# A new order of the items of phase one in a fused attention and MoE kernel

## The chip, the core and the metric

The kernel runs on one core of a Trainium2 chip. The metric is the time of one execution on the device in microseconds. All operands are f32. The engines are called by their names in the profile: PE is TensorE (matmuls; PEld is its weight loads), DVE is VectorE, ACT is ScalarE, POOL is GpSimd and SP is SyncE, which here only issues DMA transfers.

## The reference: what is computed

Attention with pooled keys and values, whose output is the input of an "act-snake" layer. There are 8 batches, 8 heads, 576 positions and 64 values a head; the layer has 4608 tokens, a model width of 512 and an inner width of 2048.

```python
k_p = k.reshape(B, H, Sp, pool, D).mean(axis=3)          # pool = 8, Sp = 72
v_p = v.reshape(B, H, Sp, pool, D).mean(axis=3)
scores = scale * np.matmul(q, k_p.transpose(0, 1, 3, 2))
scores = scores - np.max(scores, axis=-1, keepdims=True)
attn = np.exp(scores)
attn = attn / (np.sum(attn, axis=-1, keepdims=True) + 1e-09)
x = np.matmul(attn, v_p)                                 # heads side by side: 4608 x 512
h = x @ w_in                                             # 512 x 2048
g = h + np.sin(alpha * h) ** 2 / (alpha + 1e-09)
out = g @ w_out                                          # 2048 x 512
```

## The kernel before

**Two phases.** Phase one (to some 509 us) computes attention and g and writes g to a tensor in HBM, `g_bridge`. Phase two reads g back and multiplies it with w_out; its code is `outputs`, its matmuls stand at L1294.

**Phase one: units and groups.** The tokens are taken in nine units u of 512. In each unit there are four groups J, one for each quarter of the inner width; group number n is 4u + J. A group computes its part of h by a scheme of Strassen's kind: seven products M1 to M7 of sums of blocks of x and w_in instead of eight, each in four parts ("M5.2" is a part; one matmul call of 128 x 128 weights and 256 columns at L975, which PE runs as two instructions). Four PSUM banks collect them. "c16" and "c67" are ACT copies from one bank into another (L950), because a later product is added to an earlier sum; "p5" is an ACT copy of M5's bank into SBUF. DVE forms the other blocks of h ("a00", "a01", "a11", L949). ACT applies the sine ("s00", "s01", "s10", "s11", L1044, two instructions each) and squares ("q00", "q01", "q1", L1051), DVE adds the square to h ("f10", "f1", L949), and SP stores the group's g with two DMAs of 512 KB ("st", L1099).

In units 1 to 6, except in the first group of unit 1, some products (M5 for J = 0, 2, 3; M1 for every J) are themselves computed by seven smaller products: items "i.a" to "i.e5". PE's parts of these are matmuls of 128 columns at L1066; between them ACT copies ("i.ca" L1079, "i.cm" L1083, "i.cb" L1086) and one DVE add ("i.ad", L1089). The order of dependence is i.a, then i.ca and i.cm, then i.b, i.cb, i.d, then i.ad, which reads the bank that i.d has finished, and then i.e1 and i.e5, which add to what i.ad wrote.

**Attention, spread between the groups.** While unit u's groups run, the attention of batch u + 1 and the loads for batch u + 2 go along, item by item (`carry`). The items of one batch:

- load_k0, load_k1 (L261, 576 KB each), load_v (L280 and L285), load_q (L224, L245): DMAs on SP's queue. pool_k0, pool_k1, pool_vm, pool_v: sums of 8 rows on POOL (L271).
- qa, qb, qc: DVE transposes of q, 32 by 32 (L357, L360). qd, qe: eight DMAs each on SP that move the transposed blocks to their partitions (L370, `q<-tr`). k_t and k_c: a PE transpose of the pooled k and its DVE copies (L402, L406).
- scores0, scores1: PE's products of q and k (L444). shift0 to shift3: DVE maximum and subtraction (L464, L465). exp0 to exp3: ACT (L490). norm0 to norm3: DVE and POOL (L496 to L498).
- turn0 to turn3: DVE transposes of the weights (L630 to L636). move: sixteen DMAs on SP (L650, `ex<-tr`). values: PE's products with v (L739, L752). out0 to out4: ACT writes the result into x (L666). sx0 to sx3: DVE differences of blocks of x (L939) for M5, M6, M7 and M4 of the next unit. inner_x: such differences for the inner products, on POOL (L931).

Unit 0 carries the end of batch 0 and batch 1, with items of its own; there the differences are called sn0 to sn3.

**What sets the order.** The kernel sets the order by hand. Each item has a slot in a table, and a key is made of it; a list of all items is sorted by key and performed in that order, and each engine's queue holds its instructions as they come. Nothing reorders them afterwards: an engine that waits for one instruction holds all that stand behind it. Semaphore waits follow from the data.

```python
self.at(7 * n + where[m], f)          # group n: where = ORDER[self.kind(n)]
at(ORDER["U"][name], f)               # unit u: key 28 * u + slot
self.agenda.sort(key=lambda x: x[:2])
```

So four groups of 7 fill a unit of 28, and slots can be below 0 or above 7: parts of neighbouring groups interleave. The tables: "U" is the unit's items for u from 1 on, "U0" those of unit 0, "F" the first batch, "U7" the differences in the last but one unit, "R" the preparation of phase two and its first steps ("o0" to "o2", the start of `outputs`, whose key is 224 plus the slot; so "o1" is at 249.65, where the last group, number 35, has its slot 4.65). The groups' tables are chosen by `kind`: "first0" to "first3" for unit 0, "enter" for the first group of unit 1, "mid0" to "mid3" for the other groups up to unit 6, "exit" for the last group of unit 6, "end0" to "end3" for units 7 and 8.

Of the kernel before, what the change touches and what calls it, by code (L numbers as in the profile page):

```python
# [46 lines left out]
    "load_q": 13.4176, "load_k1": 13.54022, "turn0": 15.964, "move": 24.04575, "clean": 24.12855, "qa": 24.12869, "values": 24.12873,  # L47
    "out4": 24.12875, "qb": 24.12884, "pool_k1": 24.12885, "out0": 24.12885, "mark": 24.12895, "qc": 24.129, "out2": 24.129, "sx0": 24.1291,
    "inner_x": 24.12915, "out3": 24.33175, "k_t": 24.4364, "k_c": 24.4956, "qd": 24.83712, "out1": 24.87145, "sx1": 24.87995, "qe": 24.96216,
    "sx2": 25.5786, "sx3": 33.62096},  # L50
# [56 lines left out]
"enter": {  # L107
# [6 lines left out]
"exit": {  # L114
    "i.a": -5.02158, "i.ca": -4.768, "i.cm": -4.76115, "i.b": -4.15145, "i.cb": -3.5502, "i.d": -3.09985, "i.ad": -3.09835, "i.e1": -2.6215,
# [1455 lines left out]
```

## Time and profile before

| | us |
|---|---|
| median of 3 runs (904.27 to 905.8) | 905.39 |
| span of the profiled execution | 902.2 |
| PE busy | 894.0 |
| PEld busy (beside PE) | 815.0 |
| DVE busy | 678.2 |
| ACT busy | 457.3 |
| POOL busy | 206.5 |

The profiled execution's span runs from its first to its last instruction; the timed runs are 3.2 us longer in the median, which is start and end outside of the span. Busy times of the engines lie beside each other. The profile page's chain of waits goes back from the last instruction to what released it; a group's row gives busy time, mean duration in ns and idle time before it with the releaser; a line of the waits gives the waiting engine, line and tile, the releaser, the sum in us, the count and the longest. In a timeline a line has start, duration, engine, line, tiles, count. SPq lines are DMA issues; their duration is the time to issue, not to land.

In stages of about 55 us, one unit each, between 134 and 409 us, PE is busy throughout by its row, DVE 35.9 to 39.4 us, ACT 42.3 to 44.0 and POOL 16.6 to 23.6 us, the DMA engines 0.52 to 0.70 of the time. The granted PE clock is 1.00 in all of them.

### The profile page before, as it was taken

How to read it: one execution, taken by the hardware profiler on the slowest of the kernel's cores; microseconds unless marked ns; L12 is line 12 of the kernel's file. 1: busy time of each engine (PE TensorE's matmuls, PEld its weight loads, DVE VectorE, ACT ScalarE, POOL GpSimd, SP SyncE). 2: the span in 40 equal slices, each digit the busy share in tenths (PEclk: the TensorE clock that was granted, in tenths of full speed). 3: DMA queues.
4: the chain of work that ended last, by engine and by line, in shares of the span. 5: the costliest groups of instructions: out<-in, count | busy, mean ns of one | idle time of the engine just before them, and what ended most of it. 6: DMA issues, size and time to landing. Idle time of an engine off the chain costs nothing.

```text
span 902.2 us, 18350 instructions
## 1 busy us (share of the span) xinstructions
PE 894.0 (99%) x7146; PEld 815.0 (90%) x7146; DVE 678.2 (75%) x1016; ACT 457.3 (51%) x1073; POOL 206.5 (23%) x235
## 2 busy tenths in 40 slices
PE   8999999999999999999999999999999999999997
PEld 5787888978888898888888899999999999999997
DVE  7576857668586684854466999979798888889894
ACT  5696878868787787786885611211111111111111
POOL 4969561814418164130000000000000000000000
PEclk9999999999999999999999999999999999999999
DMA  9956766666766666645426346261618172534401
GB/s 271 229 170 181 209 193 177 209 173 200 212 179 197 198 187 173 175 133 200 181 104 213 99 152 193 65 191 35 224 30 231 31 201 63 171 92 130 134 15 40
DMA packets 128751, 141.17 MB, mean 156 GB/s; under 512 B 46920, under 2 KB 95704, under 8 KB 128664
## 3 DMA queue, kind: packets, MB, share of 16 engines
q1 hardware_dynamic: 125880, 137.88, 52.6%
q10 hardware_dynamic: 2784, 2.11, 0.9%
q8 instruction: 57, 0.93, 0.4%
q14 instruction: 30, 0.25, 0.1%
HBM read 75.37 MB, written 47.19 MB: 136 GB/s over the span
## 4 chain that ended last, share of the span: by engine, by line
PE 98%; DVE 1%; DMA 0%; ACT 0%; issue 0%; ACTq 0%
PE PS L1294 43%; PE PS L975 41%; PE PS L1066 7%; PE PS L444 2%; PE PS L739 2%; PE PS L752 1%; DVE home L939 1%; DMA q<-in_q_dram 0%; PE PS L553 0%; PE PS L532 0%; PE PS L1131 0%; PE PS L416 0%; PE PS L697 0%; PE PS L343 0%; PE PS L695 0%; PE PS L607 0%
## 5 line engine op out<-in xcount | busy, mean ns | idle before, releaser
L975 PE MATMUL PS<-home,a 128*128 128x256 f32 x968 | 250.3, 382 | 0.0
L975 PEld LDWEIGHTS PS<-home,a 128*128 128x128 f32 x968 | 177.3, 190 | 28.6 <-issue 4.7
L975 PE MATMUL PS<-home,as 128*128 128x256 f32 x728 | 194.9, 381 | 0.9 <-DVE home L939 0.9
L975 PEld LDWEIGHTS PS<-home,as 128*128 128x128 f32 x728 | 134.1, 190 | 18.3 <-DVE home L939 0.9
L1294 PE MATMUL PS<-s,wb 128*128 128x144 f32 x896 | 119.1, 286 | 0.0
L1294 PEld LDWEIGHTS PS<-s,wb 128*128 128x128 f32 x896 | 113.6, 190 | 0.0
L1051 ACT ACTIVATE s<-s,c 128x256 f32<-128x256 f32 (+1 forms) x216 | 112.7, 580 | 0.0
L1344 POOL TENSOR_TENSOR cc<-cc,cb 128x576 f32<-128x576 f32 x1 | 2.0, 1974 | 483.1 <-DVE cb L1249 483.1
L949 DVE TENSOR_TENSOR h<-PS,s 128x512 f32<-128x512 f32 x72 | 49.5, 687 | 70.3 <-ACT s L1051 70.3
L1430 ACT COPY PS<-PS 128x144 f32<-128x144 f32 x56 | 14.7, 263 | 143.4 <-PE PS L1294 140.8
L1294 PE MATMUL PS<-r,wb 128*128 128x144 f32 x512 | 73.2, 286 | 0.0
L1294 PE MATMUL PS<-s,a 128*128 128x144 f32 x512 | 73.2, 286 | 0.0
L1044 ACT ACTIVATE s<-h,al 128x256 f32<-128x256 f32 x144 | 64.1, 502 | 16.4 <-DVE h L949 13.3
L271 POOL TENSOR_TENSOR kvin<-kvin 96x768 f32<-96x768 f32 (+3 forms) x42 | 69.9, 1665 | 3.1 <-DMA a<-in_moe_w_in_dram 0.6
L1294 PEld LDWEIGHTS PS<-r,wb 128*128 128x128 f32 x512 | 67.1, 190 | 0.1
L1294 PEld LDWEIGHTS PS<-s,a 128*128 128x128 f32 x512 | 67.1, 190 | 0.0
L949 DVE TENSOR_TENSOR h<-PS,p 128x512 f32<-128x512 f32 x72 | 49.1, 685 | 22.3 <-PE PS L975 21.7
L950 ACT COPY PS<-PS 128x512 f32<-128x512 f32 x72 | 41.4, 576 | 46.2 <-PE PS L975 23.0
L1044 ACT ACTIVATE s<-PS,al 128x256 f32<-128x256 f32 x144 | 60.3, 473 | 6.1 <-PE PS L975 5.8
L498 POOL TENSOR_TENSOR ex<-ex,sm 128x576 f32<-128x576 f32 (+1 forms) x28 | 35.2, 1270 | 109.8 <-DVE sm L497 108.9
L1412 ACT COPY PS<-PS 128x144 f32<-128x144 f32 x56 | 14.7, 263 | 88.7 <-PE PS L1294 88.7
L949 DVE TENSOR_TENSOR h<-h,s 128x1024 f32<-128x1024 f32 x36 | 44.8, 1246 | 14.2 <-ACT s L1051 14.1
(217 smaller groups left out, 1531.4 us busy)
## 6 DMA issues: line engine op xcount, KB each, us to landing
g_bridge<-h SPq DMA_DIRECT2D x72, 512.0 KB
r<-g_bridge SPq DMA_DIRECT2D x31, 1152.0 KB
out_dram<-o SPq DMA_DIRECT2D x122, 72.0 KB
kvin<-in_k_dram SPq DMA_DIRECT2D x14, 576.0 KB
q<-in_q_dram SPq DMA_DIRECT2D x7, 1024.0 KB
kvin<-in_v_dram SPq DMA_DIRECT2D x14, 512.0 KB
ex<-tr SPq DMA_DIRECT2D x54, 92.0 KB
ex<-tr SPq DMA_DIRECT2D x54, 88.0 KB
```

The source lines that it names most:

```text
L271: self.nc.gpsimd.tensor_tensor(out=t[..., 0:w] if w > D else out, in0=t[..., 0:w], in1=t[..., w:2 * w], op=OP.add)
L444: nc.tensor.matmul(ps[e][r0 + r:r0 + r + q.shape[-1], h, :], q[s], kb[s, hp, :], start=True, stop=True)
L498: nc.gpsimd.tensor_tensor(out=E(i), in0=E(i), in1=sm.unsqueeze(2).to_broadcast([P, n, Sp]), op=OP.mult)
L739: nc.tensor.matmul(o[r:r + 64], w, x, start=start and i < 2, stop=False, skip_group_check=True)
L949: add = lambda o, x, y: nc.vector.tensor_tensor(out=o, in0=x, in1=y, op=OP.add)
L950: copy = lambda o, x: nc.scalar.copy(out=o, in_=x)
L975: nc.tensor.matmul(ps[:, jj, :], self.A[p][:, kk, f * P:(f + 1) * P], x[:, kk, :], start=start and p not in G.begun, stop=(kk == 1), skip_ ...
L1044: self.nc.scalar.activation(out=G.s()[:, i, jj, j, :], in_=src[:, jj], func=AF.Sin, scale=self.al[:, f:f + 1])
L1051: self.nc.scalar.activation(out=x, in_=x, func=AF.Square, scale=self.c[:, f:f + 1])
L1066: nc.tensor.matmul(out, W[m][:, G.J], self.X2[p][m], start=start, stop=True, skip_group_check=True)
L1294: nc.tensor.matmul(out, W[:, J // 2, J % 2, :], A[:, J, :], start=(start and J == 0), stop=(J == self.NJ - 1), skip_group_check=True)
L1412: nc.scalar.copy(out=st["x1"][:, 1, :], in_=st["x1"][:, 0, :])
```

## The change

Only numbers in the table ORDER are new: those of "U", "end0" to "end3", "enter", "exit", "first0" to "first3" and "mid0" to "mid3". Names, operations, tiles and transfers stay. "F" (the first batch), "U0", "U7" and "R" keep their numbers. The program has the same instructions in both versions, 541 DMAs on SP and 13 on ACT, apart from the waits on semaphores between them (PE 254 and then 252, ACT 291 and 279, DVE 321 and 330, POOL 111 and 110, SP 181 and 184). The changed file is ten lines longer within the table, so that L975 becomes L985 and so on.

Two of the places in words. In "U" the DMA moves qd and qe, both at about 24.9 before, stand at 24.3 and 29.1: between them now come two stores ("st" of a group) and load_k0 of the next batch (at -2.8 of the next unit, 25.2 here). In "mid3" and "exit" as in the others, i.e1 and i.e5 stand further behind i.ad than they did.

```diff
 "U": {
-    "load_k0": -3.59252, "load_v": -0.96965, "scores0": 3.279, "shift1": 6.66681, "shift0": 7.14828, "scores1": 7.66855, "shift2": 7.69635,
...
-    "load_q": 13.4176, "load_k1": 13.54022, "turn0": 15.964, "move": 24.04575, "clean": 24.12855, "qa": 24.12869, "values": 24.12873,
-    "out4": 24.12875, "qb": 24.12884, "pool_k1": 24.12885, "out0": 24.12885, "mark": 24.12895, "qc": 24.129, "out2": 24.129, "sx0": 24.1291,
-    "inner_x": 24.12915, "out3": 24.33175, "k_t": 24.4364, "k_c": 24.4956, "qd": 24.83712, "out1": 24.87145, "sx1": 24.87995, "qe": 24.96216,
-    "sx2": 25.5786, "sx3": 33.62096},
+    "load_k0": -2.8250723, "scores0": 0.5857662, "shift1": 1.0717224, "shift0": 1.0827303, "scores1": 8.3882114, "shift2": 10.4991635,
+    "exp1": 11.165643, "exp0": 11.5859082, "shift3": 11.616854, "pool_k0": 11.626981, "exp2": 11.6269842, "exp3": 11.7278035, "load_v": 11.7293126,
...
+    "load_k1": 11.9490121, "turn3": 12.0644122, "turn1": 12.6257197, "load_q": 12.8268737, "pool_k1": 15.0669519, "clean": 15.0933368,
+    "pool_vm": 15.8286396, "pool_v": 17.866474, "move": 20.672534, "qb": 22.3496327, "qc": 24.0548236, "values": 24.0585347, "mark": 24.0662953,
+    "out4": 24.0671002, "out0": 24.0979304, "qa": 24.0981694, "out2": 24.0985162, "out3": 24.1565579, "sx0": 24.2086769, "k_t": 24.2853448,
+    "k_c": 24.2950439, "inner_x": 24.2968397, "qd": 24.3191907, "out1": 24.3619433, "sx1": 24.5667552, "sx2": 25.1581598, "qe": 29.1248421,
+    "sx3": 29.1312358},
...
 "end3": {
...
-    "M4.2": 4.2433, "M4.0": 4.41961, "M4.3": 4.42479, "s01": 4.63625, "s10": 4.64555, "q01": 6.26891, "q1": 6.5869, "f1": 6.76776, "f10": 7.38579,
-    "st": 10.05},
...
+    "q01": 4.3173274, "M4.2": 4.6452332, "s10": 4.64555, "q1": 4.6470475, "f1": 6.6621497, "f10": 7.4423293, "st": 8.2738671},
 "enter": {
-    "M1.0": -0.5012, "M1.2": -0.49378, "M1.1": -0.48667, "M1.3": -0.47146, "M5.0": -0.45225, "M5.1": -0.39509, "M5.2": -0.11055, "M5.3": -0.01999,
-    "c16": 0.2794, "p5": 0.86945, "M6.0": 2.04465, "M2.0": 2.65792, "M2.1": 4.32577, "M2.3": 4.65506, "M6.1": 4.856, "M6.3": 4.86001, "M6.2": 4.87325,
...
+    "M1.0": -0.2046709, "M1.3": -0.1478548, "M1.1": -0.1446769, "M1.2": -0.046174, "c16": -0.0136544, "M5.0": 0.4150293, "M5.3": 0.420676,
+    "M5.1": 0.4360173, "M5.2": 0.4717303, "M6.0": 0.4900667, "p5": 0.5493729, "M6.1": 0.5625392, "M6.3": 1.0762283, "M2.0": 1.79859,
...
 "mid0": {
-    "i.a": -3.44775, "i.ca": -3.11535, "i.cm": -3.1115, "i.b": -3.11065, "i.cb": -3.1106, "i.d": -2.748, "i.ad": -1.9601, "i.e5": -0.69805,
-    "p5": 2.55425, "i.e1": 2.87235, "c16": 2.92563, "M2.3": 5.96454, "M2.2": 5.96455, "M2.0": 5.96456, "M6.2": 5.96456, "M6.1": 6.07936,
...
+    "i.a": -3.6916192, "i.ca": -3.3128811, "i.b": -3.0311432, "i.cb": -2.951107, "i.cm": -2.8418044, "i.d": -2.8417678, "i.ad": -2.8042301,
+    "i.e5": 0.0539427, "i.e1": 0.0748215, "p5": 0.0963461, "c16": 0.5698113, "M2.2": 0.9641797, "M2.3": 0.9877027, "M2.1": 1.0895164,
...
 "exit": {
-    "i.a": -5.02158, "i.ca": -4.768, "i.cm": -4.76115, "i.b": -4.15145, "i.cb": -3.5502, "i.d": -3.09985, "i.ad": -3.09835, "i.e1": -2.6215,
-    "i.e5": -2.5921, "c16": -1.98745, "M6.3": -1.6521, "M6.1": 1.03682, "M2.1": 1.99737, "M6.2": 2.6094, "M2.0": 2.6097, "M6.0": 2.61059,
...
+    "i.a": -5.7170466, "i.ca": -5.1713547, "i.b": -4.2359372, "i.cb": -3.8379418, "i.d": -3.8159482, "i.cm": -3.7995184, "i.ad": -2.9857453,
+    "i.e1": -0.6667843, "c16": -0.2461357, "i.e5": -0.2165688, "M6.2": -0.2019642, "M6.3": -0.1979378, "M2.0": -0.189832, "M6.0": 0.0901443,
...
 "mid3": {
-    "i.a": -5.44769, "i.cm": -5.07042, "i.ca": -4.6089, "i.b": -4.1596, "i.cb": -3.09295, "i.d": -3.08935, "i.ad": -3.08745, "i.e1": -2.73575,
...
+    "i.a": -5.8347122, "i.ca": -5.1713514, "i.cm": -4.8365744, "i.b": -4.1342384, "i.cb": -4.1048847, "i.d": -3.4866891, "i.ad": -3.2781619,
+    "i.e1": -0.8431389, "c16": -0.3116682, "i.e5": -0.2224887, "M6.2": -0.2202882, "M6.0": 0.2738904, "p5": 2.6316117, "M6.1": 2.6333881,
...
```

More of the change, by code (lines that the diff above doesn't have):

```diff
@@ L80 @@
 "end0": {
[26 rows of a table removed]
-"enter": {
[6 rows of a table removed]
-"exit": {
-    "i.a": -5.02158, "i.ca": -4.768, "i.cm": -4.76115, "i.b": -4.15145, "i.cb": -3.5502, "i.d": -3.09985, "i.ad": -3.09835, "i.e1": -2.6215,
[34 rows of a table removed]
-    "i.a": -3.44775, "i.ca": -3.11535, "i.cm": -3.1115, "i.b": -3.11065, "i.cb": -3.1106, "i.d": -2.748, "i.ad": -1.9601, "i.e5": -0.69805,
[6 rows of a table removed]
-    "i.a": 4.34025, "i.ca": 4.3997, "i.cm": 4.40437, "i.b": 4.4051, "i.cb": 4.40681, "M5.0": 4.41522, "i.d": 4.41525, "i.ad": 4.61795,
[6 rows of a table removed]
-    "i.a": -2.3038, "i.cm": -1.76102, "i.ca": -1.7514, "i.b": -1.7503, "i.cb": -1.7501, "i.d": -1.735, "i.ad": -1.59855, "i.e1": -1.0348,
[6 rows of a table removed]
-    "i.a": -5.44769, "i.cm": -5.07042, "i.ca": -4.6089, "i.b": -4.1596, "i.cb": -3.09295, "i.d": -3.08935, "i.ad": -3.08745, "i.e1": -2.73575,
[5 rows of a table removed]
[27 rows of a table added]
+"enter": {
[7 rows of a table added]
+"exit": {
+    "i.a": -5.7170466, "i.ca": -5.1713547, "i.b": -4.2359372, "i.cb": -3.8379418, "i.d": -3.8159482, "i.cm": -3.7995184, "i.ad": -2.9857453,
[37 rows of a table added]
+    "i.a": -3.6916192, "i.ca": -3.3128811, "i.b": -3.0311432, "i.cb": -2.951107, "i.cm": -2.8418044, "i.d": -2.8417678, "i.ad": -2.8042301,
[7 rows of a table added]
+    "i.a": 4.1556036, "i.ca": 4.3387363, "i.b": 4.3596664, "i.cm": 4.503322, "M5.0": 4.5236076, "i.cb": 4.6105216, "i.d": 4.6269693,
[7 rows of a table added]
+    "i.a": -2.2706958, "i.cm": -2.1707003, "i.ca": -2.0398794, "i.b": -2.0163978, "i.cb": -1.8551907, "i.d": -1.2779286, "i.ad": -1.1683365,
[7 rows of a table added]
+    "i.a": -5.8347122, "i.ca": -5.1713514, "i.cm": -4.8365744, "i.b": -4.1342384, "i.cb": -4.1048847, "i.d": -3.4866891, "i.ad": -3.2781619,
[6 rows of a table added]
 }
```

156 rows, old and new, of the table ORDER are left out of this document.

## The prediction

> **What bounds the kernel now.** I read the head of the page and its chain first, then the waits of TensorE and of its weight loads, then the timeline where a wait stands.
>
> ```profile
> span 902.2 us, 18350 instructions
> ...
> PE 894.0 (99%) x7146; PEld 815.0 (90%) x7146; DVE 678.2 (75%) x1016; ACT 457.3 (51%) x1073; POOL 206.5 (23%) x235
> ...
> PE 98%; DVE 1%; DMA 0%; ACT 0%; issue 0%; ACTq 0%
> ...
> L975 PE MATMUL PS<-home,a 128*128 128x256 f32 x968 | 250.3, 382 | 0.0
> ```
>
> TensorE is the bound: 98% of the chain. An f32 matmul runs as two passes, and their starts in the timeline lie 216 ns apart (four of L975 in 0.86 us), so one part of an M product, two matmuls of 256 columns at L975 or four of 128 at L1066, costs 0.43 us whatever its place. The change adds no pass and takes none away. What it can move are holes in the TensorE stream, and those are small: over all of phase one I count 9.9 us of them between starts. The sum is made against the span of 902.2; the median of the three runs, 905.39, is 3.2 more, which lies outside the span and which I leave as it is.
>
> The waits of TensorE's weight loads name the holes:
>
> ```profile
> PEld PS L739 <- issue: 6.7, 27, 0.3
> ...
> PEld PS L1066 <- DVE PS L1089: 4.2, 11, 0.4
> ...
> PEld PS L975 <- ACT PS L950: 1.4, 7, 0.2
> ```
>
> ```profile
> 127.33 1.03 PE L975 MATMUL PS<-home,a 128*128 128x256 f32 x4
> 128.34 0.49 PE L1066 MATMUL PS<-home,aM 128*128 128x128 f32 x2
> 128.66 0.39 PE L1066 MATMUL PS<-ex,a 128*128 128x128 f32 x2
> ```
>
> The second fence (TensorE's timeline) prices one of the eleven: four matmuls from 127.33 should let the next start at 128.19, it starts at 128.34, and its pair takes until 128.66 instead of 128.56. That is 0.15 + 0.10 = 0.25 us; the weight-load row counts more because loads run ahead.
>
> **Gain a, the inner products.** In six units the DVE add L1089 ("i.ad") releases "i.e1" and "i.e5" of L1066. Before, two M parts (the four matmuls from 127.33, 0.86 us) stand between "i.d", whose end starts the add (0.70 us), and the readers. In the new order of TensorE there are three at each of the eleven places. The third is 0.43 us, more than the 0.15 that is missing, and leaves 0.3 spare. 11 x 0.247 = -2.7 us; bounds -2.7 and -1.5, should five of the adds start later behind other DVE work.
>
> **Gain b, copies c67.** Seven waits on L950, each showing 0.06 us on the starts, and one of 0.25 us on an output copy (L666) near 84.5 lose their late releaser. I take -0.6; bounds -0.9 and -0.2.
>
> **Loss c, values.** The new slot puts "values" (L739) directly behind the group's copy p5 (L950, ACT): laid on the rows' durations, the copy ends 0.09 us after TensorE arrives, where it ended 0.27 us ahead. Five units at 0.09 to 0.2 (a lateness costs about 0.1 more, as at 128.34): +0.7, bounds 0 and 1.0. In unit 0 the same comes from copies L666 and L746, 0.32 and 0.09 late: +0.45, bounds 0 and 0.6.
>
> **Loss d, i.ca.** The copy L1079 comes 40 ns ahead of its reader instead of 250; rows with 35 to 75 ns of cover show 0.04 to 0.09 us. Six times 0.05: +0.3, bounds 0 and 0.6.
>
> **Loss e, the first group of unit 1 (near 85 to 92 us).**
>
> ```profile
> 85.02 4.05 DVE L939 TENSOR_TENSOR home<-home 128x512 f32<-128x512 f32 x2 [1.68 <-ACT home L666]
> 89.00 1.75 DVE L939 TENSOR_TENSOR home<-home,home 128x512 f32<-128x512 f32 x1
> ```
>
> ```profile
> 87.45 1.13 PE L975 MATMUL PS<-home,as 128*128 128x256 f32 x4 [0.54 <-DVE home L939]
> ...
> 90.89 0.67 PE L975 MATMUL PS<-home,as 128*128 128x256 f32 x2 [0.33 <-DVE home L939]
> ```
>
> Four differences of x (L939) run one after another beside POOL's sums and take 2.38, 1.75, 1.75 and 1.34 us, where they take 0.69 alone. M5 and M6 of "enter" wait for them. The new table lays an add L949 (0.69) between the first difference and the others, and M6.0 right behind the four parts of M5 (2.04 to 0.49), so 1.7 us of TensorE's work that stood between is gone. By the rows: M5 late 0.15 instead of 0.61, M6 1.62 instead of 0.51; +0.6, bounds 0 and 1.6.
>
> **Loss f, into phase two.**
>
> ```profile
> 514.34 0.38 ACT L1397 COPY PS<-PS 128x288 f32<-128x288 f32 x1
> 514.64 2.13 ACT L1051 ACTIVATE s<-s,c 128x256 f32<-128x256 f32 x4
> ...
> 516.67 0.27 ACT L1430 COPY PS<-PS 128x144 f32<-128x144 f32 x1
> ```
>
> The last group's "q1" moves from slot 6.587 to 4.647. Group 35 begins at key 245, so q1 goes from 251.587 to 249.647, and the first output products ("o1") are at 224 + 25.65 = 249.65: the squares now stand ahead of the copy L1397, not behind it. Its matmuls end as before, so the copy comes about 1.4 us later. One block of TensorE (0.98) has moved between, and 0.34 was spare: 0.09 late; L1430 then 0.54. +0.65, bounds 0 and 1.4.
>
> **Loss g, the moves of q.**
>
> ```profile
> 244.98 10.51 SPq L370 DMA_DIRECT2D q<-tr  x16
> 255.59 1.07 SPq L1099 DMA_DIRECT2D g_bridge<-h  x2
> 256.76 2.25 SPq L280 DMA_DIRECT2D kvin<-in_v_dram  x2
> ```
>
> ```profile
> 256.00:257.00 1.00, 1.00 (x55) 0.92 (x46) 0.91 (x3) 1.00 (x3) 0.00 (x0) 1.00 0.62 197
> 257.00:258.00 1.00, 1.00 (x6) 0.87 (x6) 0.97 (x3) 1.00 (x4) 0.00 (x0) 1.00 1.02 367
> ```
>
> SP issues the sixteen moves ("qd", "qe") in one run, 0.65 us each, then stores and loads. They land 2.0 us after issue by the trace's completions, the last near 257.0; the second half of scores that reads them begins at 260.97: 4.0 us of cover. In the new order qd begins 1.46 us later, since it waits for a DVE transpose ("qa") that has moved behind others; after its eight, SP issues the two stores (1.07 us, 1.05 MB) and load_k0 (0.55 us, 0.59 MB), and then qe. The scores move by 0.4. So by issue times alone 1.3 us of cover is left, 4.0 - 1.46 - 1.62 + 0.4. But the last columns (DMA share, GB/s) show that stores fill the engines (1.02 at 367 GB/s), and transfers of SP's queue land in order of issue: a k load issued at 238.97 landed at 244.1, stores issued behind it at 245.5 and 247.9. Stores and k are 1.64 MB: 4.5 us at 367 GB/s, 5.8 us at 281 (the row from 260 to 261). The eight moves queue up behind them, each 0.25 us of full engines (0.65 us at a share of 0.4, rows 250 to 256). In the first case the queue is empty again when the last is issued and nothing is lost; in the second it lands 1.5 us later than issue gives, 0.2 late; and if k takes the 5.1 us from issue to landing that it took at 238.97, counted from the stores' landing, up to 1.6 late. I take 0.55 late, in each of four units: +2.2, bounds 0 and 6.4.
>
> **Loss h, sx3.** The last difference of x moves from 33.6 to 29.1, beside the POOL sums of pool_k0 (L271). Beside POOL L931, L939 takes up to 1.75; beside L271 the add of two SBUF tiles runs as ever:
>
> ```profile
> L949 DVE TENSOR_TENSOR h<-h,s 128x1024 f32<-128x1024 f32 x36 | 44.8, 1246 | 14.2 <-ACT s L1051 14.1
> ```
>
> Those next to L271 took 1.215. The DVE work behind sx3 (shift L464, L465) has some 0.9 us of cover, and only then the inner products wait. +0.3 in all, bounds 0 and 4 (1.06 longer less 0.16 spare, in four to five units).
>
> The Trainium skill (SBUF — State Buffer, Who interferes with whom) says that a DVE instruction with both inputs in SBUF contends with a GpSimd instruction that reads SBUF. By that rule alone each sx3 would lose the rest of a POOL sum, and the whole change would come to some 911; the trace agrees for L939 beside L931 (1.75 against 0.69) and not for L949 beside L271 (1.215).
>
> Covered, at nothing: the pooling sums, loads of k and v and the softmax steps that move within their unit. DVE is idle about 30% and POOL more than half of each stage (windows of 55 us); their readers come a unit later. If that cover is gone, the price is one waiting stage of 0.5 us per unit, 3 us.
>
> **Sum.** -2.7 - 0.6 + 0.7 + 0.45 + 0.3 + 0.6 + 0.65 + 2.2 + 0.3 = +1.9; 905.39 + 1.9 = 907.3.
>
> **Rivals.**
> 1. The moves land in time (the other side). Loss g is nothing if stores and k go at the upper rate: -0.3, 905.1, no change. It decides as soon as the last move lands less than 1.3 us later than issue alone gives. For it: moves alone fill only 0.32 to 0.65 of the engines (250 to 257), so a block of k can be made up. Against: k loads took 5.1 us.
> 2. Gains only. If moreover the start of L739 (0.25 us in 27 rows, releaser "issue") hides loss c, and d to f come at their low ends: -3.3 + 0.9 = -2.4, 903.0. For it: the lateness of c, 0.09, is less than that start. Against: f needs 1.4 us of squares to vanish.
> 3. The queue costs its upper end. Moves 1.6 us late in four units: 907.3 + 4.2 = 911.5. For it: stores behind a k load needed 5.9 and 7.9 us to land.
> 4. sx3 is blocked. DVE's chain 0.9 late in four units: 907.3 + 3.6 - 0.3 = 910.6; rows of both signs stand above.
> 5. A cover that I count on is gone (above): 907.3 + 3 = 910.3.
>
> **Chances.** Forecast 0.38 (906 to 910, six tenths of it over 907.2), rival 1 0.20, rival 2 0.13, rival 3 0.14, rival 4 0.09, rival 5 0.06. A measurement tells 0.2%, 1.8 us, from no change. Slower by that: rivals 3 to 5 and six tenths of the forecast, 0.52. Faster: rival 2 and some of rival 1, 0.16. Within: 0.32. For 8 in 10 the range runs from just above rival 2 to just past rival 3: 903.2 to 912.0.
>
> **What would show it.** Waits of L1066 on L1089 gone (a); L739 waiting on L950 (c); in 85 to 92 us one wait of 1.6 at M6 (e); L1294 waiting on ACT L1397 and L1430 with 0.6 in all (f); the scores L444 waiting for DMA q<-tr, 0.3 to 0.8 in units 2 to 5 (g); L939 over 1 us once a unit (h). I am wrong if TensorE waits in a place that no part names, above all for pooled k or the transposes of q, or if L444 doesn't wait for DMA at all.

## The result and the profile after

The changed kernel takes 916.36 us in the median (915.36 to 917.02), the kernel before in the same runs 904.84 (904.27 to 905.8). The ratio is 1.0125, with a 95% interval of 1.011 to 1.0139: 11.5 us slower, six times the loss that was forecast (1.9 us), and outside of the range.

The head of the page and the chain of the changed kernel:

```profile
span 915.2 us, 18347 instructions
...
PE 899.5 (98%) x7146; PEld 820.9 (90%) x7146; DVE 687.2 (75%) x1016; ACT 455.2 (50%) x1073; POOL 206.4 (23%) x235
...
PE 79%; DVE 6%; ACT 5%; DMA 4%; SPq 2%; issue 1%; POOL 1%; ACTq 0%; DVEq 0%; POOLq 0%
```

TensorE is still the bound, but only 79% of the chain runs through it where it was 98%; DVE, ACT and DMA have come in. Line numbers are ten higher than before: L985 was L975, L959 was L949.

Its waits, first of the matmuls, then of the weight loads (waiting engine, line, tile, releaser, sum in us, count, longest):

```profile
PE PS L985 <- ACT PS L960: 4.0, 4, 1.2
...
PE PS L454 <- DMA q<-tr: 0.9, 2, 0.6
...
PE PS L1304 <- ACT PS L1440: 0.4, 1, 0.4
PE PS L1304 <- DVE r L1259: 0.3, 1, 0.3
PE PS L1304 <- DVE x L1259: 0.3, 1, 0.3
```

```profile
PEld PS L1076 <- ACT PS L1089: 2.7, 6, 0.5
...
PEld PS L1076 <- DVE PS L1099: 0.3, 1, 0.3
```

The last line is gain a: of eleven waits for the add "i.ad" (4.2 us in the weight-load row before) one is left. The first line is new and was in no part of the prediction: TensorE waits about a microsecond for the copy "c16" (L960, from bank to bank), four times.

Where the time between the two profiled executions goes, from the starts of the matmuls (lateness against the same step elsewhere, the 0.1 us that follows a wait included where it could be separated):

| | us |
|---|---|
| c16: 1.09, 1.21, 0.95, 1.41, 0.27 in five units | +4.9 |
| i.ca (L1089): five times 0.37 | +1.9 |
| second half of scores, units 2 to 5: blocks of 2.85, 2.16, 2.39, 2.19 where they took 1.55 | +3.4 |
| values, units 1 to 5: blocks of 4.52, 3.87, 3.87, 3.88, 3.87 where they took 3.5 to 3.6 | +2.4 |
| values, unit 0: a block of 4.00 where it took 3.42, between starts | +0.6 |
| phase two, first to last matmul: 386.26 instead of 384.10 | +2.2 |
| i.ad: one of eleven waits left | -2.5 |
| first group of unit 1: one wait, 0.77 with its tail, instead of two, 1.38 | -0.6 |
| c67 and the output copy near 84.5 | -0.6 |
| sum | +11.7 |

From the first product to the first matmul of phase two the time rose from 491.6 to 501.2 us, which with phase two makes 11.7. The spans differ by 13.0, because the first product came 1.6 us later in this execution. That isn't the kernel's doing: in the executions profiled for this study it comes at 21.6 to 23.4 us where the order of the kernel before is the base, and at 21.4 to 23.5 where the changed one is. The timed runs lie 1.7 to 2.1 us above their spans, so of the 3.2 us that were put outside of the span before, more than 1 was the difference of that execution from the median; the difference between the kernels doesn't hang on it.

**What makes c16 late.** The timeline of DVE and of POOL around one of these waits, in the changed kernel:

```profile
229.97 0.69 DVE L959 TENSOR_TENSOR h<-PS,p 128x512 f32<-128x512 f32 x1
230.58 3.15 DVE L959 TENSOR_TENSOR h<-h,s 128x1024 f32<-128x1024 f32 x1
233.66 0.68 DVE L959 TENSOR_TENSOR h<-PS,s 128x512 f32<-128x512 f32 x1
```

```profile
229.79 0.43 POOL L516 MEMSET ex<- 32x128 f32 x2
230.30 4.56 POOL L281 TENSOR_TENSOR kvin<-kvin 128x1024 f32<-128x1024 f32 x2
```

and the same place before, again DVE and POOL:

```profile
225.64 1.22 DVE L949 TENSOR_TENSOR h<-h,s 128x1024 f32<-128x1024 f32 x1
```

```profile
225.14 0.61 POOL L291 TENSOR_TENSOR vz<-vr,mask 128x256 f32<-128x256 f32 x1
225.71 3.37 POOL L271 TENSOR_TENSOR kvin<-kvin 128x1024 f32<-128x1024 f32 x1
```

The add "f1" (h plus the squares, both inputs in SBUF) and the first sum of pool_vm (1024 columns, both inputs in SBUF) don't run side by side. Alone they take 1.22 and 2.35 us. Before, f1 starts 0.07 us ahead of POOL: f1 takes 1.22 and POOL's sum 3.37. After, POOL starts 0.28 us ahead of f1: POOL takes its 2.35 (4.56 is two sums), and f1 takes 3.15. Before, f1 led by 0.06 to 0.08 us in four units running. After, it was behind by 0.42, 0.28, 0.56 and 0.09 us in units 1, 3, 4 and 5 and took 3.02, 3.15, 2.88 and 3.34 us. In unit 6 it was behind by 1.23 and took 2.21; that is the unit with the 0.27 us of c16. In unit 2 f1 led by 0.86 us, and there neither c16 nor i.ca made TensorE wait.

The chain of the changed kernel shows how two lost microseconds on DVE come to TensorE:

```profile
230.03 3.71 DVE h L959 x2
233.77 0.64 ACT s L1054 x2
234.58 1.61 ACT s L1054 x4
236.19 1.23 ACT s L1061 x2
237.42 0.48 ACT PS L960
```

Sines and squares on ACT wait for DVE, the copy c16 stands behind them on ACT, and the matmul at 237.95 has waited 1.05 us for it.

**The moves of q**, on SP and then on TensorE, in unit 3:

```profile
195.90 4.67 SPq L380 DMA_DIRECT2D q<-tr  x7
200.62 1.12 SPq L1109 DMA_DIRECT2D g_bridge<-h  x2
201.84 0.84 SPq L271 DMA_DIRECT2D kvin<-in_k_dram  x1
202.72 6.83 SPq L380 DMA_DIRECT2D q<-tr  x8
```

```profile
210.00 0.84 PE L454 MATMUL PS<-kblk,q 64*64 64x72 f32 x34
211.13 1.00 PE L454 MATMUL PS<-kblk,q 64*64 64x72 f32 x46 [0.30 <-DMA q<-tr]
```

The eight last moves are issued behind stores and k, in 6.83 us where eight took some 5.2 before, and the scores stop in mid-block for them.

**Into phase two**, the chain of the changed kernel (pieces of it):

```profile
527.22 0.30 ACT PS L1407
...
528.93 8.38 DMA r<-g_bridge
537.31 0.02 issue
537.33 2.57 DVE x L1259
```

Behind the copies that the prediction named there is a load of r on ACT's own DMA queue. It goes out at 528.93, 4.6 us after phase two's first matmul; before it was at 516.37, 3.2 us after. DVE's sums and then two blocks of TensorE wait for it.

### The profile page after: what moved, and what is told of

Read it like the earlier page. It is cut to its first block, busy times and chain, and to the rows that moved or that the text cites. A ratio compares the mean times of both kernels' runs of the same rounds, so it can differ in the third digit from the quotient of the medians.

```text
span 915.2 us, 18347 instructions
## 1 busy us (share of the span) xinstructions
PE 899.5 (98%) x7146; PEld 820.9 (90%) x7146; DVE 687.2 (75%) x1016; ACT 455.2 (50%) x1073; POOL 206.4 (23%) x235
## 4 chain that ended last, share of the span: by engine, by line
PE 79%; DVE 6%; ACT 5%; DMA 4%; SPq 2%; issue 1%; POOL 1%; ACTq 0%; DVEq 0%; POOLq 0%
PE PS L1304 40%; PE PS L985 29%; PE PS L1076 4%; DVE h L959 3%; ACT s L1054 2%; PE PS L454 2%; DMA kvin<-in_k_dram 2%; ACT s L1061 2%; PE PS L749 1%; SPq L660 1%; SPq L380 1%; DMA r<-g_bridge 1%; POOL kvin L281 1%; PE PS L762 1%; DVE tr L640 1%
## 5 line engine op out<-in xcount | busy, mean ns | idle before, releaser
L985 PE MATMUL PS<-home,a 128*128 128x256 f32 x968 | 249.6, 381 | 4.1 <-ACT PS L960 4.0
L985 PEld LDWEIGHTS PS<-home,a 128*128 128x128 f32 x968 | 179.1, 190 | 32.1 <-ACT PS L960 5.1
L985 PE MATMUL PS<-home,as 128*128 128x256 f32 x728 | 194.0, 382 | 0.5 <-DVE home L949 0.5
L985 PEld LDWEIGHTS PS<-home,as 128*128 128x128 f32 x728 | 132.5, 190 | 17.5 <-ACT s L1054 0.9
L1304 PE MATMUL PS<-s,wb 128*128 128x144 f32 x896 | 119.2, 286 | 0.4 <-ACT PS L1440 0.4
L1304 PEld LDWEIGHTS PS<-s,wb 128*128 128x128 f32 x896 | 113.6, 190 | 0.6 <-ACT PS L1440 0.6
L959 DVE TENSOR_TENSOR h<-PS,s 128x512 f32<-128x512 f32 x72 | 48.7, 687 | 69.1 <-ACT s L1061 69.0
L281 POOL TENSOR_TENSOR kvin<-kvin 96x768 f32<-96x768 f32 (+3 forms) x42 | 71.9, 1712 | 44.0 <-DMA kvin<-in_k_dram 41.4
L959 DVE TENSOR_TENSOR h<-h,s 128x1024 f32<-128x1024 f32 x36 | 52.5, 1458 | 33.4 <-ACT s L1061 33.4
L1304 PE MATMUL PS<-r,wb 128*128 128x144 f32 x512 | 73.3, 286 | 0.3 <-DVE r L1259 0.3
L1304 PE MATMUL PS<-s,a 128*128 128x144 f32 x512 | 73.2, 286 | 0.0
L1304 PEld LDWEIGHTS PS<-r,wb 128*128 128x128 f32 x512 | 67.1, 190 | 0.6 <-DVE r L1259 0.6
L1304 PEld LDWEIGHTS PS<-s,a 128*128 128x128 f32 x512 | 67.0, 190 | 0.0
L960 ACT COPY PS<-PS 128x512 f32<-128x512 f32 x72 | 41.5, 576 | 45.7 <-PE PS L985 22.6
L959 DVE TENSOR_TENSOR h<-PS,p 128x512 f32<-128x512 f32 x72 | 48.7, 684 | 13.5 <-PE PS L985 12.1
L1304 PE MATMUL PS<-x,wb 128*128 128x144 f32 x384 | 55.0, 286 | 0.3 <-DVE x L1259 0.3
```

The lines of the kernel that those rows point to most:

```text
L281: self.nc.gpsimd.tensor_tensor(out=t[..., 0:w] if w > D else out, in0=t[..., 0:w], in1=t[..., w:2 * w], op=OP.add)
L959: add = lambda o, x, y: nc.vector.tensor_tensor(out=o, in0=x, in1=y, op=OP.add)
L960: copy = lambda o, x: nc.scalar.copy(out=o, in_=x)
L985: nc.tensor.matmul(ps[:, jj, :], self.A[p][:, kk, f * P:(f + 1) * P], x[:, kk, :], start=start and p not in G.begun, stop=(kk == 1), skip_ ...
L1304: nc.tensor.matmul(out, W[:, J // 2, J % 2, :], A[:, J, :], start=(start and J == 0), stop=(J == self.NJ - 1), skip_group_check=True)
```

## Experiments

Each kernel is measured against the kernel before in the same job; "before" below is that job's median. Ratios carry their 95% interval.

**POOL's order alone.** The short sums of pool_v go ahead of the long ones of pool_vm, as they did in the kernel before.

```diff
-"pool_vm": 15.8286396, "pool_v": 17.866474,
+"pool_vm": 17.866474, "pool_v": 15.8286396,
```

> The changed kernel with two POOL items exchanged: the short sums of v's last rows (pool_v) ahead of the long sums (pool_vm). Theory (port): the add f1 (L959, two inputs in SBUF, 1.2 us alone, 2.2 to 3.3 us in five units) is held by the 2.35 us sum of pool_vm that began just before it, and the waits of PE for the copies c16 (L960, 4.9 us in sum) and for i.ca (L1089, five of 0.37 us) come of that. Then f1 meets only sums of some 0.5 us and those waits go: 4 to 7 us faster than the changed kernel, some 910 to 912 us. Rival (order): ACT and DVE are late through the new places of the transposes turn0 to turn3, and f1 only waits where something else would: no change, 915 to 917 us.

910.08 us, before 905.51; ratio 1.0052 (1.0039 to 1.0065). f1 takes 1.6 us at most, where it meets the short sums, as here, on DVE and on POOL:

```profile
228.63 1.60 DVE L959 TENSOR_TENSOR h<-h,s 128x1024 f32<-128x1024 f32 x1
```

```profile
228.43 2.52 POOL L281 TENSOR_TENSOR vr<-vr 128x256 f32<-128x256 f32 x3
```

No wait for c16 is left, and of those for i.ca two of 0.04 us and less. The time from first product to phase two falls by 6.6 us. The transposes turn0 to turn3 stand where the change put them, so the rival falls: it is the meeting of the two instructions, not their place in ACT's or DVE's order as such.

**One transpose alone, on the kernel before.** Why did f1 lose its lead? In the changed kernel the 0.9 us of turn0 stand ahead of it, and POOL's two items have changed places. The next kernel does only the first of these to the kernel before.

```diff
-"turn0": 15.964,
+"turn0": 12.95,
```

> The kernel before with one transpose moved as the change moves it: turn0 ahead of the add f1 of mid0, so that f1 comes 0.9 us later on DVE. Theory (who starts first holds the port): before, f1 starts 0.06 to 0.08 us ahead of the 2.35 us sum of pool_vm in four units and takes 1.22 us; now POOL starts first, f1 takes 2.5 to 3.3 us, and PE waits about 1 to 1.5 us a unit for a copy that hangs on it: 4 to 7 us slower than before, 909 to 912 us. Rival (only 0.9 us later): f1's readers have that much cover; less than 1.5 us slower.

915.83 us, before 905.67; ratio 1.0116 (1.0102 to 1.013). One item moved by 0.9 us costs 10.2 us, more than expected. DVE, POOL and TensorE:

```profile
232.24 2.75 DVE L949 TENSOR_TENSOR h<-h,s 128x1024 f32<-128x1024 f32 x1
```

```profile
231.55 4.57 POOL L271 TENSOR_TENSOR kvin<-kvin 128x1024 f32<-128x1024 f32 x2
```

```profile
237.97 0.70 PE L975 MATMUL PS<-home,as 128*128 128x256 f32 x2 [1.21 <-ACT PS L950]
```

f1 is 0.09 us behind POOL in unit 1 and 0.68 in units 2 to 5, takes 3.35 and 2.75 us, and TensorE is 1.97 us late for the copy L950 in unit 1 and 1.38 in each of the others. The rest are seven waits of 0.2 us for the same line, and the 0.1 us that follows each.

**The same with POOL out of the way.**

```diff
-"turn0": 15.964, "pool_v": 11.93269,
+"turn0": 12.95, "pool_v": 11.93271,
```

> The same as the run with turn0 first, and pool_vm ahead of pool_v on POOL, so that its 2.35 us sum is over when f1 starts and f1 meets a sum of 1.27 us half done at most. Theory (port): f1 takes below 1.9 us; at least 3 us faster than with turn0 first alone, 905 to 907.5 us. Rival (0.9 us later): the same time as with turn0 first.

910.22 us; ratio 1.0049 (1.0037 to 1.0062). Against the run before it 5.6 us come back: f1 takes 1.20 in unit 1 and 1.8 in units 2 to 5, where it now starts behind the second sum of pool_vm (512 columns, 1.27 us alone), and TensorE waits 0.43 there instead of 1.38. DVE and POOL (the second sum starts at 227.27):

```profile
227.83 1.79 DVE L949 TENSOR_TENSOR h<-h,s 128x1024 f32<-128x1024 f32 x1
```

```profile
224.83 3.71 POOL L271 TENSOR_TENSOR kvin<-kvin 128x1024 f32<-128x1024 f32 x2
```

Of the 10.2 us, at least 5.6 are thus the held add. The other 4.6 are the 0.9 us of transposes in a place without cover and the 0.6 us for which f1 is still held; this run doesn't separate them. The theory's 905 to 907.5 us was missed, and the rival of that pair may be right for a part.

**The order on SP alone.** qe directly behind qd.

```diff
-"qe": 29.1248421,
+"qe": 24.3192,
```

> The changed kernel with the eight moves qe directly behind qd, ahead of the two stores and of load_k0. Theory (queue): the second half of the scores waits 0.6 to 1.3 us in four units because the moves stand behind 1.64 MB of stores and k on one queue; then these waits go and the kernel is 3.4 us faster, some 913 us. Rival (late start): qd and qe are late because the DVE transpose qa comes later; then at least half of the waits stay, 914.5 us or more.

908.73 us, before 905.51; ratio 1.0038 (1.0026 to 1.005). All second halves of the scores take 1.55 us again, here at the place shown above:

```profile
208.15 1.53 PE L454 MATMUL PS<-kblk,q 64*64 64x72 f32 x80
```

That is the 3.4 us, and the rival falls, since qd begins as late as in the changed kernel (14.6 us ahead of this block in both). The gain was larger, 7.6 us between the medians and 6.1 in the profiled execution (the twelve runs spread from 905.67 to 910.9), because with SP's order POOL's start moved too: f1 led by 0.61 and 0.21 us in units 4 and 5 and took 1.2 us there.

**ACT's order alone.** q1 of end3 behind the first output products.

```diff
-"q1": 4.6470475,
+"q1": 6.5869,
```

> The changed kernel with q1 of end3 back at slot 6.587, behind the first output products. Theory (ACT's queue): both the copies L1407 and L1440 and the load of r that ACT issues behind them come earlier; the waits of PE for the copies (1.0 us) and for x and r of L1259 (1.2 us) all go: 2.2 us faster, some 914.2 us. Rival (copies alone): the load of r is late through the stores on SP; only the 1.0 us goes, 915.4 us.

914.58 us, before 905.51; ratio 1.0096 (1.008 to 1.0111). Phase two takes 384.19 us again, 2.07 less, and all four waits of L1304 are gone. The load on ACT's queue goes out 3.3 us after the first matmul of phase two, as before:

```profile
527.55 0.26 ACT L1440 COPY PS<-PS 128x144 f32<-128x144 f32 x1
527.58 0.40 ACTq L1250 DMA_DIRECT2D r<-g_bridge  x1
```

**Three parts undone together** (pool_v ahead, qe ahead, q1 back).

> The changed kernel with three parts undone: pool_v ahead of pool_vm, qe directly behind qd, q1 of end3 behind the first output products. Sine and square stay ahead of values. Theory: the waits for i.ca that the run with four parts undone showed (4 us) came of putting sine and square behind values, so they are gone here, and port, queue and ACT's order explain nearly all of the loss: 903 to 906 us, within 0.2% of the kernel before. Rival: those waits stay, 908 us or more.

904.98 us, before 905.53; ratio 0.9993 (0.9984 to 1.0002). The three parts explain the whole loss. Alone they had given back 6.3, 7.6 and 1.8 us, more than the loss together, because the run with SP's order had also freed the add in two units. What remains of the change is worth 1.1 us from first product to phase two (490.5 instead of 491.6) and can't be told from nothing.

**Sine and square behind values**, alone and with the three parts undone:

```diff
@@ mid2 @@
-"s01": 9.635832, "q01": 10.0469423,
+"s01": 10.059, "q01": 10.06,
@@ first3 @@
-"s00": 5.3159962, "q00": 5.4449274,
+"s00": 5.5515, "q00": 5.6186,
```

> The changed kernel with sine and square of mid2 (s01, q01) and of first3 (s00, q00) behind the item values on ACT, ahead of which they stand now. Theory: PE's values wait for the small copy L756 (order) that stands behind 1.8 us of sine and square on ACT; the blocks of values take 3.51 us again instead of 3.87 to 4.52: 1.5 to 3 us faster than the changed kernel, 913.4 to 915 us. Rival: the copy p5 (L960) sets the end; no change.

> The changed kernel with four parts undone together: pool_v ahead of pool_vm, qe directly behind qd, q1 of end3 behind the first output products, and sine and square behind values. Theory: the four losses add up (6.3 + 3.4 + 2.0 + 2.2 us) and what stays are the gains: L1076's waits for L1099 gone (2.7), the copies (0.6), one wait of enter (0.5): 901 to 903 us, faster than the kernel before by 2 to 4 us. Rival: with these undone the waits for i.e1 and i.e5 or new ones come back, 904 us or more.

Both missed. Alone it gave 924.96 us (ratio 1.0221, 1.0201 to 1.0242), 8.6 us worse than the changed kernel, and most of that in the second halves of the scores, where the waits for the moves of q grew from 0.9 to 6.3 us:

```profile
PE PS L454 <- DMA q<-tr: 6.3, 9, 1.4
```

With the three parts undone it gave 909.34 us (ratio 1.0039, 1.0027 to 1.0052): 1.28, 0.80, 0.43, 0.41 and 1.17 us and three of 0.1 to 0.2 for i.ca. The blocks of values still took 3.86 to 4.17 us. With the square alone moved it was 905.03 us (ratio 0.9996, 0.9987 to 1.0005), and values took 3.87 and more:

> The same with only the square q01 of mid2 behind the small copy L756 (order), the sine ahead of it. Theory: the copy then comes 0.9 us earlier and the blocks of values take 3.51 us again, while ACT idles less than 0.2 us: 1.5 to 2 us faster than with three parts undone. Rival: what stands behind on ACT is late by as much as values gain; no gain.

So the small copy L756 isn't what values waits for.

**p5 ahead of the squares**, with the three parts undone:

```diff
@@ mid3 @@
-"p5": 2.6316117,
+"p5": 0.25,
```

> The run with three parts undone, and p5 of mid3 ahead of the squares q1 on ACT (slot 0.25 in place of 2.63). Theory (loss c as predicted): values starts 0.23 us late because the copy p5 (L960) ends just ahead of it, and 0.1 us follows; with p5 1.3 us earlier the blocks take 3.51 us in five units and the kernel is 1.8 us faster than with three parts undone, 902.5 to 904 us, 0.15 to 0.3% below the kernel before. Rival: the squares, 0.6 us later, delay adds and stores, and nothing is won: 904.5 us or more.

904.02 us, before 905.63; ratio 0.999 (0.9981 to 0.9999). The interval only just leaves out 1, and the profiled execution, at 905.5 one of the slower ones, shows no gain: 876.0 us from the first product to the last matmul, where the kernel before took 875.7. So a gain over the kernel before is hardly shown. The wait at the start of values is gone in three of five units, but the blocks still take 3.86 to 4.08 us; the stop is now in mid-block. What holds values there, some 2 us in all, stays open.

**Gain a alone**, on the kernel before: one more M part ahead of i.e1 and i.e5.

```diff
@@ mid3 @@
-"M4.3": 10.06132, "i.e1": -2.73575,
+"M4.3": 4.4636, "i.e1": -2.55,
@@ exit @@
-"i.e1": -2.6215, "i.e5": -2.5921,
+"i.e1": -2.555, "i.e5": -2.55,
```

> The kernel before with gain a alone: one more M part between the end of i.d and the readers i.e1 and i.e5 at the eleven places where PE waited for the add L1089 (M4.3 of mid3 and i.e1, i.e5 of mid3 and exit moved). Theory: each place gives 0.25 us, 2.7 us faster than before, some 902.1 us. Rival: the waits move to the next copy or add and less than 1 us is won, 904 us or more.

909.22 us, before 905.51; ratio 1.0036 (1.0024 to 1.0049): 3.7 us slower, not 2.7 faster. The waits on L1089 are gone, and others have come:

```profile
PE PS L975 <- ACT PS L950: 2.9, 7, 1.3
PE PS L444 <- ACT p L950: 1.4, 5, 0.3
```

The part that now stands ahead of i.e1 had stood behind it and covered the next copy: c16 is 0.42 us late in six units, and the scores 0.33 us in five. And in unit 2 f1 fell 0.11 us behind POOL, took 3.32 us, and TensorE waited 1.34 us there.

**The tables enter and end alone**, on the kernel before.

> The kernel before with only the tables enter and end0 to end3 of the change (q1 of end3 at its old slot). Theory: in enter one wait of 0.7 us in place of two (1.4 us with what follows them), in the end groups five bumps of 0.06 us less: 0.5 to 1.2 us faster than before, within 0.2%. Rival: the moved stores of end1 and end2 come late for phase two, slower by 1 us or more.

913.3 us (ratio 1.0085, 1.0071 to 1.0099), but this mixture of tables computes something else in group 4: the sine of the next group overwrites a square that "f10" of enter has yet to read (key 35 + 7.84 for that sine, 28 + 15.03 for f10). TensorE waits up to 3.7 us for i.ca at the seam of the two tables. It says nothing of enter by itself.

## Why the prediction was wrong

**The step that failed is "Covered, at nothing", with loss h behind it.** It put the pooling sums and the softmax steps that move within their unit at nothing and counted the idle time of DVE and POOL; the transposes turn0 to turn3 it didn't name at all. What counted was which of two instructions starts first, and a lead of 0.07 us can't be seen in shares of busy time. The moved transpose and the moved sums cost c16's 4.9 and i.ca's 1.9 us; exchanging two POOL items brings back 6.6 of them.

The evidence against contention was misread. "Those next to L271 took 1.215" holds for the adds that had started first, and there the price stood in the partner's row: POOL's sum took 3.37 us instead of 2.35. Two adds of the same profile had started behind a sum of L271, by 1.06 and 0.82 us, and took 1.83 and 1.54 us. The first of them, on DVE and POOL, in the kernel before:

```profile
78.68 1.83 DVE L949 TENSOR_TENSOR h<-h,s 128x1024 f32<-128x1024 f32 x1
```

```profile
77.62 3.75 POOL L271 TENSOR_TENSOR kvin<-kvin 96x768 f32<-96x768 f32 x2
```

So both orders stood in the profile before. The prediction looked for the delay only in instructions that had won. Where the Trainium skill (SBUF — State Buffer, Who interferes with whom) says that a DVE instruction with two SBUF inputs contends with a GpSimd instruction that reads SBUF, and that the order of issue and not the shape decides who is blocked, the traces agree with both: 1.22 and 3.37 us with DVE ahead, 3.15 and 2.35 with POOL ahead. The 911 that the prediction worked out by that rule was for sx3; the place was another.

**Loss g** was right in its mechanism and its place, too small in size: the row was 0.55 us in each of four units, and measured were 1.30, 0.61, 0.84 and 0.64, 3.4 us instead of 2.2.

**Loss f** had the two copies right and their size too small (0.65 forecast; 0.37 and 0.67, together 1.0, measured), and it left out a DMA: the load of r stands behind the copy L1430 on ACT. With it the loss was 2.2 us.

**Loss c** was mis-sized: 0.7 forecast for five units, 2.4 measured, of which 0.6 in unit 1 hangs on the held add. That p5 is the releaser is only partly borne out by the last run with p5 ahead. In unit 0 0.6 stood against 0.45; no experiment moved it.

**Loss d**, 0.3 forecast, was 1.9, but as a follower of the held add: with POOL's items exchanged the copy is on time.

**Loss e** had the wrong sign: the two waits of the first group became one of 0.7 us, a gain of 0.6. The differences of x were no longer held as long: the first took 1.22 us beside POOL, where it had taken 2.38.

**Gain a and gain b** came as forecast (2.5 and 0.6 us). As an argument gain a was incomplete: the run of it alone shows that the part placed ahead of one reader is taken from another's cover. In the changed kernel other parts had moved as well.

**Loss h** itself, sx3 beside pool_k0, did take 1.6 to 2.2 us in three units. The scores that follow wait for the moves of q there; with qe ahead, sx3 no longer met POOL. Its own price couldn't be separated.

Rival 4 named the mechanism, with a chance of 0.09 and for another instruction; rival 5 named the step, with 3 us.

## What to carry to other kernels

Where two engines may want the same resource, compare their start times in the trace, and read the durations of both: a lead of 0.07 us that repeats in every unit can turn into a price as soon as a change delays the leader. When an order is changed, list for each moved item the instructions that share an engine or a DMA queue with it or were seen to hold it up, and for each cover that is spent once, ask whose cover it was. A table of slots that fits is a system: of its parts, one moved alone cost 10 us and another, meant to remove a wait, 3.7.

## What was not expected of the hardware

An add of 1.22 us on DVE (two SBUF inputs, 128 x 1024) takes 2.75 to 3.38 us when a POOL sum of 2.35 us (128 x 1024) has begun 0.05 to 0.7 us before it, and 2.21 us when it has begun 1.23 us before; each time it ends about 1.1 us after that sum. When DVE begins 0.06 to 0.08 us ahead, DVE's duration is unchanged and POOL's sum takes 3.36 to 3.38. Shorter sums hold the add for less time: behind one of 1.27 us (128 x 512), begun some 0.55 us before it, it took 1.8 us, and behind one of 0.73 us (128 x 256), begun 0.03 to 0.49 us before it, 1.8 to 1.3.
